# Products over the whole TensorE array, earlier weight conversions and experts in a written order, in a fused attention, gated FFN and mixture-of-experts kernel

## The chip, the core and the metric

The kernel runs on one core of one Trainium2 chip. The core has five engines with an instruction queue each: TensorE (PE, matrix products; its loads of the stationary operand are listed as PEld), VectorE (DVE), ScalarE (ACT), GpSimd (POOL) and SyncE (SP, which here only issues DMA transfers). An engine works through its queue in order, and instructions of different engines are tied together by semaphores. The metric is the device time of one execution. Before the change it is 1046.84 us, the median of three runs (1045.98, 1046.84 and 1047.32). All times below are microseconds (us) unless a nanosecond is named.

## The reference

Three stages, each feeding the next, in fp32:

```
x = attention(q, k, v)        # 4 batches x 8 heads x 576 positions x 64, block-causal (blocks of 64)
x = x as [2304, 512]          # 4*576 tokens
x = (sigmoid(x @ w_gate) * (x @ w_val)) @ w_out       # 512 -> 1536 -> 512
logits = x @ moe2_w_gate                              # 8 experts
# capacity assignment: walk all (token, expert) pairs in descending order of logit;
# a token takes the expert if it has none yet and the expert holds fewer than 288 tokens
out[tokens of e] = relu(x[tokens of e] @ w1[e]) @ w2[e]      # 512 -> 1024 -> 512, 288 tokens each
```

## The kernel before

Every large fp32 product is made of three faster ones: both operands are split into a high part and the rest (`xh`, `xl`, `w0h`, `w0l`, `ewh`, `ewl`: ACT writes the high part, DVE or POOL subtracts), and high x high, high x low and low x high are added up in PSUM. A PSUM tile is called `A` whatever it holds.

**Stage 1, 0 to 78 us: attention of batch 0.** Heads go in pairs; each pair takes five row blocks. PE makes scores and transposes `p`, DVE reduces maxima and sums (`stat`) and copies (`pta`, `ptb`, `kf`), ACT exponentiates, POOL scales `p` and splits the result (`xh` L218, `xl` L219). Beside it the first FFN weights are made ready (`Ffn.start`, `Ffn.convert` L339): they come as 64-bit numbers, and `ToF32` makes fp32 of one tile of 128x512 by one ACT instruction (L283) and four DVE ones (L288, L290, L292, L294). ACT and POOL then split it (`w0h` and `w1h` L357, `w0l` and `w1l` L359). `first_half` (L1115) interleaves the two generators.

**Stage 2, 78 to 573 us: the first FFN product** (L457) with the attention of batches 1 to 3 woven in. `router_weights` (L556 to L570) also computes the product w_out @ m_gate there, so that the router logits (`logits` L410, `rows` L425) come from the FFN's hidden values without waiting for its second product.

**Stage 3, 573 to 784 us: the second FFN product** (`Ffn2.run`, L683: 18 token tiles) and beside it the router. `Router.phase` (L815) finds, seven times over, a threshold for each expert by a search in two halves of three steps. A step compares all keys with J candidates (`cmp`, L840 or L845; J is 31 or 63 or 64), counts on PE by 18 products of `cmp` with the one-hot experts `oh` (L824, bf16, J columns of the array), makes flags on DVE (`ge` L831), and adds them up on PE (L834, J rows of the array, and in the last step of a phase L837). `FILL` says how many L683 products stand between. The output rows go to DRAM through `x2r` (L690) as two halves of 256 columns.

**Stage 4, 784 to 1044 us: the experts.** For each: POOL fetches the expert's tokens by indirect DMA (`gather` L997, three token tiles of 128, 128 and 32, two halves each, one expert ahead), `xtrans` (L1009) transposes them on PE, L1049 is the product with w1, L1090 that with w2, `ytrans` (L1023) transposes the result back, and POOL scatters it by three indirect DMAs (L1030). Eight weight chunks per expert are loaded by SP into `eraw` (3 buffers) and split by `split` (L958: `ewh` on ACT, two instructions `ewl` on DVE or POOL, in turn) into a ring of 5. In this version all of stage 4 goes through the scheduler, which places each instruction by its own costs; the code order is only a hint.

## Time and profile before

| | us |
|---|---|
| median of three runs | 1046.84 |
| the profiled execution | 1045.71 |
| its span, first to last instruction | 1044.0 |
| PE busy | 993.2 (95%) |
| DVE, ACT, POOL busy | 587.7, 449.7, 507.4 (56%, 43%, 49%) |
| mean granted TensorE clock | 0.985 of full |

The span is what the trace covers; the device time is 1.7 us longer. A busy share says little on its own: PE is busy 95% of the span, so that a change has to take work from PE, or one of its few waits, to move the time. A timeline row gives the start, the duration from start to end, and in brackets how long the engine was idle before and which instruction it waited for. PE's products overlap in the pipeline: the time that one costs is the distance from its start to the next start, not its duration.

### The profile page before, as it was taken

What the parts mean: (1) busy time and instruction counts of PE and PEld (TensorE: products, weight loads), DVE (VectorE), ACT (ScalarE), POOL (GpSimd) and SP (SyncE); (2) the same over time, 40 slices, a digit from 0 to 9 for tenths busy, and PEclk for the clock granted to TensorE, in tenths of its full rate; (3) what the DMA queues carried; (4) which work ended last, traced back from release to release, by engine and by line L of the source; (5) the groups of instructions that cost most, each with busy time, mean ns of one, the idle gap of its engine ahead of it and who ended that gap; (6) DMA issues with size and microseconds to landing.
All of it is one profiled execution on the core that took longest, in us unless ns stands there. A gap on an engine that the chain in (4) does not pass through costs nothing.

```text
span 1044.0 us, 19724 instructions
## 1 busy us (share of the span) xinstructions
PE 993.2 (95%) x7387; PEld 858.1 (82%) x7387; DVE 587.7 (56%) x1385; ACT 449.7 (43%) x1069; POOL 507.4 (49%) x519
## 2 busy tenths in 40 slices
PE   7979999999999999999999999999997999999995
PEld 4658888788888888899999766666687999999995
DVE  5887889477666455435685566655631434434441
ACT  5765565355554455434554222111121444444541
POOL 3663444433333334532324677765645666666441
PEclk9989999999999999998999999999998999999998
DMA  6556666556454322236665543433312665555540
GB/s 170 141 130 176 203 199 178 181 165 185 142 184 119 96 68 79 75 98 226 207 210 157 148 126 102 119 84 96 98 47 63 205 186 174 177 169 183 185 127 23
DMA packets 188527, 148.89 MB, mean 143 GB/s; under 512 B 70800, under 2 KB 161424, under 8 KB 188432
## 3 DMA queue, kind: packets, MB, share of 16 engines
q1 hardware_dynamic: 184848, 138.20, 44.5%
q0 software_dynamic: 3584, 9.44, 2.8%
q8 instruction: 58, 0.95, 0.4%
q14 instruction: 37, 0.30, 0.1%
HBM read 114.57 MB, written 33.03 MB: 141 GB/s over the span
## 4 chain that ended last, share of the span: by engine, by line
PE 84%; DVE 8%; issue 4%; POOL 1%; ACT 1%; SPq 1%; DMA 0%; POOLq 0%; another core or an unknown queue 0%; ACTq 0%; DVEq 0%
PE A L457 29%; PE A L683 12%; PE A L1049 10%; PE A L1090 9%; PE A L211 5%; PE A L116 4%; PE A L163 4%; PE A L824 2%; PE A L410 2%; DVE sub L811 2%; PE A L122 2%; PE A L1009 1%; PE A L85 1%; DVE cmp L840 1%; DVE hl L512 1%
## 5 line engine op out<-in xcount | busy, mean ns | idle before, releaser
L151 POOL TENSOR_SCALAR p<-p,stat 128x128 f32<-128x128 f32 (+2 forms) x144 | 81.2, 576 | 191.1 <-DVE stat L149 135.8
L359 POOL TENSOR_TENSOR w0l<-wf,w0h 128x512 fp32r<-128x512 f32 x48 | 67.0, 1395 | 136.9 <-ACT w0h L357 103.4
L457 PE MATMUL A<-xh,w0h 128*128 128x288 f32 x384 | 121.6, 317 | 2.6 <-ACT w0h L357 2.6
L457 PE MATMUL A<-xh,w1h 128*128 128x288 f32 x384 | 122.1, 318 | 1.9 <-ACT ptb L168 1.9
L976 POOL TENSOR_TENSOR ewl<-eraw,ewh 128x512 fp32r<-128x512 f32 x68 | 90.2, 1345 | 63.1 <-ACT ewh L969 55.6
L457 PE MATMUL A<-xh,w0l 128*128 128x288 f32 x384 | 114.5, 298 | 3.7 <-POOL w0l L359 3.7
L457 PE MATMUL A<-xh,w1l 128*128 128x288 f32 x384 | 114.3, 298 | 0.0
L457 PE MATMUL A<-xl,w1h 128*128 128x288 f32 x384 | 114.3, 298 | 0.0
L457 PE MATMUL A<-xl,w0h 128*128 128x288 f32 x384 | 114.1, 297 | 0.0
L969 ACT ACTIVATE ewh<-eraw 128x1024 fp32r<-128x1024 f32 x64 | 67.8, 1060 | 67.2 <-PE A L1090 42.0
L124 DVE TENSOR_REDUCE stat<-A 128x1 f32<-128x128 f32 (+4 forms) x160 | 70.4, 477 | 44.2 <-PE A L122 20.5
L683 PE MATMUL A<-wo_h,hl 128*128 128x512 f32 (+1 forms) x240 | 95.0, 396 | 0.0
L683 PE MATMUL A<-wo_l,hh 128*128 128x512 f32 (+1 forms) x240 | 92.1, 384 | 0.0
L660 POOL TENSOR_TENSOR hl<-hraw,hh 128x512 fp32r<-128x512 f32 x54 | 75.8, 1426 | 28.7 <-ACT hh L656 28.7
L683 PE MATMUL A<-wo_h,hh 128*128 128x512 f32 (+1 forms) x240 | 89.7, 374 | 0.0
L974 DVE TENSOR_TENSOR ewl<-eraw,ewh 128x512 fp32r<-128x512 f32 x60 | 48.6, 851 | 70.8 <-ACT ewh L969 64.9
L138 ACT ACTIVATE p<-A,stat 128x128 f32<-128x128 f32 (+4 forms) x160 | 81.8, 520 | 11.7 <-DVE stat L124 7.5
L690 ACT ACTIVATE x2r<-A 128x512 f32<-128x512 f32 (+1 forms) x20 | 11.1, 555 | 168.2 <-PE A L683 162.6
L1049 PE MATMUL A<-exh,ewh 128*128 128x288 f32 x256 | 75.9, 314 | 6.0 <-issue 3.3
L457 PEld LDWEIGHTS A<-xh,w1h 128*128 128x128 f32 x384 | 73.5, 191 | 9.0 <-issue 5.1
L457 PEld LDWEIGHTS A<-xh,w0h 128*128 128x128 f32 x384 | 73.1, 190 | 8.7 <-issue 4.4
L1049 PE MATMUL A<-exl,ewh 128*128 128x288 f32 x256 | 75.8, 299 | 2.3 <-issue 2.3
(219 smaller groups left out, 2717.1 us busy)
## 6 DMA issues: line engine op xcount, KB each, us to landing
eraw<-in_moe_w_dram SPq DMA_DIRECT2D x64, 512.0 KB, 3.9
wf<-wgv SPq DMA_DIRECT2D x72, 256.0 KB, 3.0
h<-h SPq DMA_DIRECT2D x48, 288.0 KB, 2.7
hraw<-h SPq DMA_DIRECT2D x16, 768.0 KB, 5.2
hraw<-h SPq DMA_DIRECT2D x12, 576.0 KB, 4.0
w<-in_moe_w_gate_dram SPq DMA_DIRECT2D x12, 512.0 KB, 4.3
w<-in_moe_w_val_dram SPq DMA_DIRECT2D x12, 512.0 KB, 4.1
wgv<-wf SPq DMA_DIRECT2D x24, 256.0 KB, 4.3
```

The lines of the kernel that those rows point to most:

```text
L124: nc.vector.tensor_reduce(st[:, x:x + 1], s[:, 0:w], axis=AX.X, op=OP.max, negate=True)
L138: nc.scalar.activation(o, s[:, 0:w], AF.Exp, bias=m, scale=1.0, accum_out=st[:, 2 + x:3 + x])
L151: self.k.mark = nc.gpsimd.tensor_scalar(t, t, r[:, x:x + 1], 1.0, op0=OP.mult, op1=OP.mult)
L211: nc.tensor.matmul(o[64 * a:64 * a + 64, b0:w], vs[0:kk, c, a, :], th[0:kk, a, c, b0:w], start=(n == 0), stop=(n == len(mm) - 1))
L359: nc.gpsimd.tensor_tensor(l, x, f32(h), op=OP.subtract)
L457: nc.tensor.matmul(o[:, 0:288], w[:, ks], x[:, ts], start=(kk == 0 and n == 0), stop=(kk == 3 and n == 2))
L660: nc.gpsimd.tensor_tensor(l[:, s], x[:, s], f32(h[:, s]), op=OP.subtract)
L683: nc.tensor.matmul(o[:, 0:b - a], x[:, f], w[:, f, a:b], start=(f == 0 and n == 0), stop=(f == 11 and n == 2))
L969: nc.scalar.activation(h, x, AF.Copy)
L976: nc.gpsimd.tensor_tensor(l[:, s], x[:, s], f32(h[:, s]), op=OP.subtract)
L1049: nc.tensor.matmul(o[:, 0:288], w[:, s], x, start=(d == 0 and n == 0), stop=(d == 3 and n == 2))
L1090: nc.tensor.matmul(o[:, 0:288], w[:, s], x, start=(n == 0), stop=(n == 23))
```

## The change

Four parts.

1. **Whole-array products.** Router counts, flags, router weights, logit rows and the third token tile of `xtrans` used 16, 31, 32, 40, 63 or 64 rows or columns of the array. Now each uses 128 x 128; what is added is zero or is not read. For this the tiles are widened and cleared once by POOL (`memset`, `affine_select`).
2. **First conversions.** `first_half` advances the weight conversion at every attention step after the second, not at every third.
3. **Experts in a written order.** Stage 4 stands under `tc.manual_schedule()`, so that its instructions keep the order of the code. The code is reordered for that: splits begin one step earlier, five of eight are split by DVE and three by POOL (four and four before); the transposes of the next expert stand in the middle of each w2 product; the back transposes and the scatters of an expert stand in the first three steps of the next one; for the last expert nine of twelve back transposes go ahead of the last product's end.
4. **Gather.** The FFN's output is stored twice, as halves (`x2_h`, which only expert 0 fetches) and as whole rows (`x2_d`). The other experts are fetched by three indirect DMAs of 2 KB rows in place of six of 1 KB rows, 128 rows each, padding included.

```diff
@@ first_half
-        n += s1.step > 2
-        if n % 3 == 1:
+        if s1.step > 2:
             next(w0, None)
@@ router_weights
-    mgs = k.const.tile([P, 4, 16], F32R, name="mgs")
+    mgs = k.const.tile([P, 4, P], F32R, name="mgs")
+    nc.gpsimd.memset(f32(mgs), 0.0)
...
-                nc.tensor.matmul(o[0:16, 0:256], mgs[:, c, :], x[:, c, :], ...)
+                nc.tensor.matmul(o[:, 0:256], mgs[:, c, :], x[:, c, :], ...)
...
-            nc.tensor.transpose(o[:, 16 * y:16 * y + 16], ot[:, P * y:P * y + P], k.ident[0:16, 0:16])
+            nc.tensor.transpose(o[:, P * y:P * y + P], ot[:, P * y:P * y + P], k.ident)
@@ Ffn2.run
-                nc.sync.dma_start(k.x2_d[c // 256][t * P:(t + 1) * P, :], y[:, c - a:c - a + 256])
+                nc.sync.dma_start(k.x2_h[c // 256][t * P:(t + 1) * P, :], y[:, c - a:c - a + 256])
+            nc.sync.dma_start(k.x2_d[t * P:(t + 1) * P, a:b], y[:, 0:b - a])
@@ Router.phase
-                    nc.tensor.matmul(o[0:J, 0:8], self.cmp[:, c * J:c * J + J], self.oh[:, c, :],
+                    nc.tensor.matmul(o[:, 0:8], self.cmp[:, c * J:c * J + P], self.oh[:, c, :],
...
-                nc.tensor.matmul(base[:, 0:1], self.wgt[h, s][0:J], self.fl[0:J], ...)
+                nc.tensor.matmul(base[:, 0:1], self.wgt[h, s], self.fl, ...)
...
-                    nc.tensor.matmul(o[:, 16:24], self.ones[0:J, :], self.ge[0:J], start=True, stop=True)
+                    nc.tensor.matmul(o[:, 16:24], self.ones, self.ge, start=True, stop=True)
@@ Experts
-EARLY = 5
+EARLY = 6
@@ xtrans
-                nc.tensor.transpose(o[:, a:b], self.gx[e, j][0:b - a, d * P:(d + 1) * P], k.ident[0:b - a, 0:b - a])
+                nc.tensor.transpose(o[:, a:a + P], self.gx[e][j][:, d * P:(d + 1) * P], k.ident)
@@ run
+                if f % 2 == 0:
+                    drain(bg)
+                    if e or f:
+                        bg = self.split("vg"[f // 2 % 2])
+                    next(bg, None)
...
-                if f % 2 == 1:
-                    drain(bg)
-                    bg = self.split("v" if f % 4 == 1 else "g")
...
-                bg = self.split("v" if d % 2 == 1 else "g")
+                bg = self.split("gv"[d % 2] if d else "v")
...
+                    if f == 3:
+                        next(nxt, None)
+                        if e == 7 and d == 3:
+                            drain(self.rows(e, yt, (0, 1, 2), False))
@@ kernel
-    ex.gather(0)
-    drain(ex.run())
+    with tc.manual_schedule():
+        ex.gather(0)
+        ex.run()
```

DVE before, in the attention of the fourth head pair of batch 0: `w` and `cv_t` rows are conversions of FFN weights, the others belong to the attention.

```order
L294 SCALAR_TENSOR_TENSOR wf_864<-w_311,cv_t 128x512
L170 COPY pta<-A 128x4x128
L146 TENSOR_SCALAR stat<-stat 128x2
L149 RECIPROCAL stat<-stat 128x2
L124 TENSOR_REDUCE stat<-A 128x1 x2
L288 TENSOR_SCALAR w_338<-w_338 128x512
L290 TENSOR_SCALAR cv_t<-cv_t 128x512
L292 SCALAR_TENSOR_TENSOR cv_t<-cv_t,w_338 128x512
L294 SCALAR_TENSOR_TENSOR wf_1035<-w_338,cv_t 128x512
L288 TENSOR_SCALAR w_381<-w_381 128x512
```

DVE now, at the first conversion, in the first head pair:

```order
L124 TENSOR_REDUCE stat<-A 128x1 x2
L288 TENSOR_SCALAR w_287<-w_287 128x512
L290 TENSOR_SCALAR cv_t<-cv_t 128x512
L170 COPY ptb<-A 128x4x128
L146 TENSOR_SCALAR stat<-stat 128x2
L149 RECIPROCAL stat<-stat 128x2
L90 COPY kf<-A 128x512
L124 TENSOR_REDUCE stat<-A 128x1 x2
L292 SCALAR_TENSOR_TENSOR cv_t<-cv_t,w_287 128x512
L294 SCALAR_TENSOR_TENSOR wf_380<-w_287,cv_t 128x512
L170 COPY ptb<-A 64x2x64
```

The four conversions of the first weights, of which two stood in a row at the end, now lie two instructions per attention step over the first three pairs; the place of the first piece in the fourth pair holds attention alone.

POOL before, in one expert (`xg` a gather, `out_dram` a scatter):

```order
L997 DMA xg_11257<-x2d_63,idx 128x256
L997 DMA xg_11257<-x2d_64,idx 128x256
L997 DMA xg_11259<-x2d_63,idx 128x256
L997 DMA xg_11261<-x2d_63,idx 32x256
L997 DMA xg_11259<-x2d_64,idx 128x256
L997 DMA xg_11261<-x2d_64,idx 32x256
L1030 DMA out_dram<-yr_10923,idx 2304x512
L1030 DMA out_dram<-yr_10970,idx 2304x512
L976 TENSOR_TENSOR ewl<-eraw,ewh 128x512 x2
L1030 DMA out_dram<-yr_11019,idx 2304x512
L976 TENSOR_TENSOR ewl<-eraw,ewh 128x512 x6
```

And now:

```order
L1011 DMA xg_10550<-x2d,idx 128x512
L1011 DMA xg_10551<-x2d,idx 128x512
L1011 DMA xg_10552<-x2d,idx 128x512
L1051 DMA out_dram<-yr_10579,idx 2304x512
L1050 MEMSET one 1x1
L1051 DMA out_dram<-yr_10580,idx 2304x512
L1050 MEMSET one 1x1
L1051 DMA out_dram<-yr_10581,idx 2304x512
L985 TENSOR_TENSOR ewl<-eraw,ewh 128x512 x6
```

Three of nine indirect DMAs and one of four splits are gone from POOL's queue, and every split stands behind all of them.

PE before, where one expert's w2 product (L1090) ends and the next expert's w1 product (L1049) begins:

```order
L1090 MATMUL A<-eh_9982,ewl 128x288
L1009 MATMUL A<-ident,xg_9858 128x128
L1009 MATMUL A<-ident,xg_9860 128x128
L1009 MATMUL A<-ident,xg_9862 128x32
L1009 MATMUL A<-ident,xg_9858 128x128
L1009 MATMUL A<-ident,xg_9860 128x128
L1009 MATMUL A<-ident,xg_9862 128x32
L1049 MATMUL A<-exh_10066,ewh 128x288
```

And now, in the middle of the last of the four w2 products (L1118):

```order
L1118 MATMUL A<-eh_9943,ewl 128x288
L1023 MATMUL A<-ident,xg_9897 128x128
L1023 MATMUL A<-ident,xg_9898 128x128
L1023 MATMUL A<-ident,xg_9899 128x128
L1118 MATMUL A<-eh_9959,ewh 128x288
```

The last transposes of the next expert's tokens no longer stand right ahead of the products that read them, and the third is as wide as the others.

## Rows read from the trace of the kernel before

**Rows 1.** The page, shares of the chain that ended last, by engine.

```profile
PE 84%; DVE 8%; issue 4%; POOL 1%; ACT 1%; SPq 1%; DMA 0%; POOLq 0%; another core or an unknown queue 0%; ACTq 0%; DVEq 0%
```

**Rows 2.** Windows (start:end length, busy us and count per engine, PE clock, DMA).

```profile
26.42:38.14 11.72, 11.72 (x93) 7.72 (x95) 8.72 (x27) 9.25 (x31) 7.28 (x14) 1.00 0.73 177
38.14:50.49 12.35, 11.79 (x93) 7.71 (x95) 11.03 (x31) 8.69 (x30) 8.07 (x13) 1.00 0.35 88
...
73.44:77.60 4.16, 4.16 (x19) 3.80 (x19) 3.41 (x6) 1.49 (x4) 1.82 (x2) 0.50 0.56 170
```

**Rows 3.** Timeline of PE at the first FFN products.

```profile
69.26 0.40 PE L457 MATMUL A<-xh,w0h 128*128 128x288 f32 x1 [2.64 <-ACT w0h L357]
...
73.44 0.61 PE L457 MATMUL A<-xh,w0l 128*128 128x288 f32 x1 [3.66 <-POOL w0l L359]
```

**Rows 4.** Timeline of POOL in the same stretch.

```profile
70.81 1.17 POOL L219 TENSOR_TENSOR xl<-xr,xh 128x320 fp32r<-128x320 f32 x1
```

**Rows 5.** Timeline of PE in a router phase, narrow products between L683.

```profile
591.72 0.74 PE L824 MATMUL A<-oneh,cmp 128*63 128x8 bf16 x18
...
592.97 0.40 PE L683 MATMUL A<-wo_l,hh 128*128 128x512 f32 x1
593.30 0.17 PE L834 MATMUL A<-flag,wgt 63*128 63x1 bf16 x1
...
593.75 0.39 PE L683 MATMUL A<-wo_h,hh 128*128 128x512 f32 x1
...
595.13 0.39 PE L683 MATMUL A<-wo_h,hh 128*128 128x512 f32 x1
595.45 0.61 PE L824 MATMUL A<-oneh,cmp 128*31 128x8 bf16 x18
...
596.33 0.40 PE L683 MATMUL A<-wo_h,hl 128*128 128x512 f32 x1
```

**Rows 6.** Timeline of PE, two whole-array bf16 products between L683.

```profile
681.39 0.39 PE L683 MATMUL A<-wo_h,hl 128*128 128x512 f32 x1
681.62 0.18 PE L863 MATMUL A<-row,ones 128*128 128x1 bf16 x1
...
682.00 0.40 PE L683 MATMUL A<-wo_l,hh 128*128 128x512 f32 x1
```

**Rows 7.** Timeline of PE, whole-array bf16 products with 48 columns moving.

```profile
765.88 0.32 PE L920 MATMUL A<-cmp,ohlo 128*128 128x48 bf16 x6
```

**Rows 8.** Waits of PE, 573 to 768 us (us in total, times, longest).

```profile
PE A L834 <- DVE ge L831: 3.9, 7, 0.7
```

**Rows 9.** Timeline of PE at the start of the experts.

```profile
788.25 1.45 PE L1049 MATMUL A<-exh,ewh 128*128 128x288 f32 x5 [2.69 <-ACT exh L1012]
...
797.70 1.05 PE L1049 MATMUL A<-exh,ewh 128*128 128x288 f32 x6 [2.22 <-issue]
```

**Rows 10.** Windows of single experts: the second and, without gathers, the sixth.

```profile
855.14:885.37 30.23, 29.50 (x219) 28.26 (x218) 12.93 (x23) 13.87 (x25) 18.91 (x18) 1.00 0.58 179
...
976.92:1006.00 29.08, 29.08 (x219) 28.17 (x218) 12.10 (x24) 14.06 (x25) 12.98 (x11) 1.00 0.54 166
```

**Rows 11.** Timeline of PE, both kinds of transposes between expert products.

```profile
875.38 0.56 PE L1009 MATMUL A<-ident,xg 128*128 128x128 f32 x3
...
876.10 0.30 PE L1090 MATMUL A<-el,ewh 128*128 128x288 f32 x1
```

**Rows 12.** The same view, the full transposes.

```profile
884.88 0.49 PE L1023 MATMUL A<-ident,yt 128*128 128x128 f32 x3
...
885.35 0.30 PE L1049 MATMUL A<-exl,ewh 128*128 128x288 f32 x1
```

**Rows 13.** Waits of PE, 784 to 1044 us.

```profile
PE A L1049 <- issue: 7.1, 12, 2.2
```

**Rows 14.** Waits of all engines, 825 to 1006 us.

```profile
ACT ewh L969 <- DMA eraw<-in_moe_w_dram: 4.0, 3, 1.8
```

**Rows 15.** Timeline of POOL, one of an expert's nine indirect DMAs.

```profile
855.11 0.97 POOL L997 DMA_INDIRECT xg<-x2d,idx  x1 [0.30 <-issue]
```

More of the change, by code (lines that the diff above doesn't have):

```diff
@@ L540, in router_weights @@
     mg = k.const.tile([P, 4, 8], F32, name="mg")
-    mgs = k.const.tile([P, 4, 16], F32R, name="mgs")
+    mgs = k.const.tile([P, 4, P], F32R, name="mgs")
+    nc.gpsimd.memset(f32(mgs), 0.0)
+    ots = [ffn.cv.tile([P, 256], F32, name=f"wot{i}", bufs=1) for i in range(2)]
+    for ot in ots:
+        nc.gpsimd.memset(ot, 0.0)
     nc.sync.dma_start(mg, k.m_gate.rearrange("(k p) e -> p k e", p=P))
@@ L555, in product @@
             for x in (xh, xl):
-                nc.tensor.matmul(o[0:16, 0:256], mgs[:, c, :], x[:, c, :], start=(c == 0 and x is xh), stop=(c == 3 and x is xl))
-        ot = ffn.cv.tile([16, 256], F32, name="wot", bufs=1)
-        nc.scalar.activation(ot, o[0:16, 0:256], AF.Copy)
+                nc.tensor.matmul(o[:, 0:256], mgs[:, c, :], x[:, c, :], start=(c == 0 and x is xh), stop=(c == 3 and x is xl))
+        ot = ots[f // 2 % 2]
+        nc.scalar.activation(ot[0:16], o[0:16, 0:256], AF.Copy)
         for _ in range(GAP):
@@ L987, in open @@
         self.hb = st.enter_context(tc.tile_pool(name="ehb", bufs=1))
+        self.one = self.hb.tile([1, 1], F32, name="one")
     def gather(self, e):
@@ L992, in gather @@
             return
[L993 removed]
+        self.gx[e] = [self.xg.tile([P, 512], F32, name=f"xg{j}") for j in range(3)]
+        for src in k.x2_h if e == 0 else (k.x2_d,):
             for j, (a, b) in enumerate(self.TOK):
[L995 to L998 removed]
+                g = self.gx[e][j]
+                if e == 0:
+                    c = k.x2_h.index(src)
+                    g = g[:, 256 * c:256 * c + 256]
+                nc.gpsimd.indirect_dma_start(out=g, out_offset=None, in_=src[:, :],
+                                             in_offset=bass.IndirectOffsetOnAxis(ap=k.idx[:, 3 * e + j:3 * e + j + 1], axis=0))
     def xtrans(self, e):
@@ L1015, in xtrans, with rows @@
             yield
-    def ytrans(self, e, yt):
+    def rows(self, e, yt, ds, copies):
         k, nc = self.k, self.k.nc
+        if not self.yo:
+            self.yo = [k.psA.tile([P, 512], F32, name="A") for _ in self.TOK]
+            self.yr = [self.yg.tile([P, 512], F32, name=f"yr{j}") for j in range(3)]
+        lo, hi = ds[0] * P, ds[-1] * P + P
         for j, (a, b) in enumerate(self.TOK):
-            n = b - a
-            o = k.psA.tile([P, 512], F32, name="A")
-            for d in range(4):
-                nc.tensor.transpose(o[0:n, d * P:(d + 1) * P], yt[d][:, a:b], k.ident)
-            r = self.yg.tile([P, 512], F32, name=f"yr{j}")
+            o = self.yo[j]
+            for d in ds:
+                nc.tensor.transpose(o[0:b - a, d * P:(d + 1) * P], yt[d][:, a:b], k.ident)
+            r = self.yr[j][0:b - a]
             if j == 0:
-                nc.scalar.activation(r[0:n], o[0:n], AF.Copy)
+                nc.scalar.activation(r[:, lo:hi], o[0:b - a, lo:hi], AF.Copy)
             else:
-                nc.vector.tensor_copy(r[0:n], o[0:n])
-            yield
-            s = nc.gpsimd.indirect_dma_start(out=k.out[:, :], out_offset=bass.IndirectOffsetOnAxis(
-                ap=k.idx[0:n, 3 * e + j:3 * e + j + 1], axis=0), in_=r[0:n, :], in_offset=None)
-            for x in self.sent:
-                k.tc.declare_no_dep(s.ins, x.ins, reason="no token is in two slots")
-            self.sent.append(s)
-            yield
+                nc.vector.tensor_copy(r[:, lo:hi], o[0:b - a, lo:hi])
+            if copies:
+                if j:
+                    nc.gpsimd.memset(self.one, 0.0)
+                s = nc.gpsimd.indirect_dma_start(out=k.out[:, :], out_offset=bass.IndirectOffsetOnAxis(
+                    ap=k.idx[0:b - a, 3 * e + j:3 * e + j + 1], axis=0), in_=r, in_offset=None)
+                for x in self.sent:
+                    k.tc.declare_no_dep(s.ins, x.ins, reason="no token is in two slots")
+                self.sent.append(s)
+            yield
+        if copies:
+            self.yo = []
     def run(self):
         k, nc = self.k, self.k.nc
+        self.yo = []
         nxt = self.xtrans(0)
-        tail, bg = iter(()), iter(())
+        tail = iter(())
         early = {}
@@ L1072, in run @@
                 next(tail, None)
[L1073 to L1075 removed]
                 next(bg, None)
+            drain(tail)
             yt = []
@@ L1096, in run @@
                 yt.append(y)
-                if d >= 1:
-                    next(nxt, None)
+            drain(bg)
             drain(nxt)
-            drain(tail)
-            tail = self.ytrans(e, yt)
-            yield
+            tail = self.rows(e, yt, range(4) if e < 7 else (3,), True)
         drain(tail)
@@ L1176, in tile_fn @@
     k.wo_d = dram.tile([12, P, 512], F32, name="wo32")
-    k.x2_d = [dram.tile([2304, 256], F32, name=f"x2d{c}") for c in range(2)]
+    k.x2_d = dram.tile([2304, 512], F32, name="x2d")
+    k.x2_h = [dram.tile([2304, 256], F32, name=f"x2h{c}") for c in range(2)]
     const = k.const = ctx.enter_context(tc.tile_pool(name="const", bufs=1))
```

37 lines of the change are left out of this document (17 added, 20 removed).

## The prediction, made before the changed kernel was run

> **What bounds the kernel now.** I read first the shares of the chain of waits: PE is 84% of it, DVE 8%, nothing else over 4% [rows 1]. So a microsecond taken off PE's queue counts, unless DVE was late in that place anyway. Then the windows, stage by stage, for PE's holes and its clock; there the reader should see that the attention pairs between 26 and 50 us keep PE full but not DVE, and that just before 77 us PE runs at clock 0.50 [rows 2]. Then PE's own timeline around the holes [rows 3, 9] and around the narrow products [rows 5, 6, 11, 12], and last the lists of what PE waits for [rows 8, 13]. The sum below is against the profiled execution, 1045.71 us, which lies 1.13 under the median of 1046.84.
>
> **1. First conversions.** PE stands 2.64 us before the first product with `w0h` and 3.66 before the first with `w0l`: 6.3 together [rows 3]. After that it runs 4.16 us at 0.50 of its clock [rows 2]; that is the lower of the two levels, after a stretch in which it had hardly worked, and costs another 2.1. The pair at 38 to 50 us lasts 12.35 in place of 11.72, with one conversion in it: 0.6 [rows 2]. In all 9.0. In the new order the four conversions are done before the fourth pair, so `w0h` is no longer late. What is late next is `w0l`: POOL has the attention's `xl` in its queue until 70.81 + 1.17 = 71.98 [rows 4], some 1 us after the second product could want it. So 8.0 can go.
>
> Against it stands DVE in the first pairs. It is busy 8.72 of 11.72 without, and 11.03 with, one conversion; a conversion is worth 2.3 [rows 2]. Two in a pair make 8.7 + 4.6 = 13.3, 1.6 more than the pair lasts, in two pairs: 3.2 if all of it reaches PE. ACT, at 9.25 [rows 2], is nearer to its limit as well. Nothing hides that, as every attention step reads DVE's sums; a part may be made good in the third pair. I take 8 - 3 = **-5**, bounds -9 (no loss) and 0 (the loss is twice as large, and a second of the waits stays).
>
> **2. Router weights and logit rows.** The 48 products with 16 columns and 12 small transposes come in six bursts each, the logit rows in four. At each border between a narrow and a wide shape PE pays what is priced in part 3, 0.1 to 0.2. Against it stands POOL, which clears two tiles once. **-1**, bounds -3 and +2 (POOL's clearing holds up the attention's `p`).
>
> **3. Router counts and flags.** A 512-column L683 takes (595.13 - 593.75)/6 = 0.23 us. From the L683 before an insertion to the second L683 after it are two of these and the insertion. So 18 products of 31 columns cost 596.33 - 595.13 - 0.46 = 0.74, and one L834 costs 593.75 - 592.97 - 0.46 = 0.32, for a product of a single column [rows 5]. Two whole-array products of that size cost 682.00 - 681.39 - 0.46 = 0.15 together [rows 6]. Thus the narrow shape, not the product, is what costs, about 0.2 at the borders. 63 columns: 0.74 within the group against 0.61 for 31 [rows 5], so 0.87.
>
> What will 18 whole-array products cost? Six of L920 lie within 0.32 [rows 7], one product within 0.18 [rows 6]: (0.32 - 0.18)/5 = 28 ns each, though 48 columns move. By the same division 31 columns cost (0.61 - 0.18)/17 = 25 ns and 63 cost 33 [rows 5]. I take 25 to 28, so 18 x 0.026 and 0.09 for the borders = 0.55. Saved: 28 groups of 31 x 0.19 = 5.3, 14 groups of 63 or 64 x 0.32 = 4.5, 42 flags x 0.22 = 9.2: 19 us of PE time, 2.7 per phase.
>
> The Trainium skill ("TensorE: Matmul & The Clock Gate", LDWEIGHTS) speaks against this: the load of the stationary operand takes time by its columns, P/1.2 ns, whatever its rows. By it 18 loads of 128 columns would be 18 x 97/1.2 = 1455 ns longer than those of 31, an estimate from that page, and the change would lose; L920's 28 ns per product [rows 7] do not agree. The same skill ("TensorEngine Tiling (Array Packing)", Key Properties) says that a change of tiling mode drains TensorE; the dearer narrow flag agrees with that.
>
> How much of the 19 reaches the end? Where PE waits for DVE, time saved before the wait only makes it longer. PE waits for `ge` seven times, 3.9 us, once per phase [rows 8]: DVE is last in one of the two halves. What is saved in that half I count as lost, the other half keeps: **-10**, bounds -19 (all of it) and -3 (DVE late in nearly every step).
>
> **4. Start of the experts.** PE stands 2.69 us for `exh` and later 2.22 [rows 9]. The first wait has a chain that stays: last `x2r`, store, gather, transpose, ACT. The second can shrink, since expert 0's second halves are no longer fetched behind expert 1's first ones, and 36 products rather than 30 lie ready. But SP has a store more per tile and the third gather is of 128 rows. **-2**, bounds -5 and +2.
>
> **5. Experts.** Three transposes with a 32-row third cost from their start to the start of the second product after them 876.10 - 875.38 = 0.72 [rows 11], three full ones 885.35 - 884.88 = 0.47 [rows 12]. There are 32 such groups: 32 x 0.25 = 8.0. PE works without a break here, so all of it counts. Besides, PE waits 7.1 us on "issue" before L1049 in twelve places [rows 13]; the sixth expert, the one without gathers, has none of it, 29.08 us against 30.23 [rows 10]. The wait lies behind POOL's indirect DMAs, 1.27 us each from one to the next [rows 15]: nine per expert are 11.4, and the splits of the first chunks queue behind them. Six make 7.6, DVE takes a fifth split and each split begins earlier: I take 4 of the 7.1 as gained. **-12**, bounds -15 and 0 (in order, ACT or POOL delays the products by what the transposes give back). An expert should last 30.2 - 1.0 - 1.0 = 28.2, or near 28.1, the 29.08 of the sixth less 1.0. The last scatters stay in the tail: 0.
>
> **Sum.** -5 - 1 - 10 - 2 - 12 = -30: 1045.7 - 30 = 1015.7 by the profiled execution, and 1.1 more against the median: 1017 us.
>
> **Rivals.**
>
> *Whole-array loads are dear.* For it: in the groups the price grows with the columns, 25 ns at 31 and 33 at 63 [rows 5]. Going on by 8 ns for 32 columns, 128 columns cost 49 ns. Then a group takes 18 x 0.049 + 0.09 = 0.97: 28 x 0.23 + 14 x 0.10 = 7.8 lost against 9.2 gained at the flags. Part 3 falls to -1: 1026. Against it: the 28 ns of L920. The Trainium skill's rule on the columns, given in part 3, points the same way, and further.
>
> *The router is DVE's.* For it: the waits of PE in each phase [rows 8], and DVE as the second on the chain [rows 1]. PE's time turns into waits in both halves, part 3 is -3: 1024. Against it: in one half no such waits are listed.
>
> *The written order stalls the experts (slower than before).* ACT must take its queue in order: `ewh` of a chunk that SP has not yet landed holds up the `eh` behind it, which frees PE's PSUM tiles and feeds the w2 product. Even before, `ewh` waited for its load three times, 1.3 us each [rows 14]. The scheduler could put another instruction first; the written order can't. With 64 chunks, the gains of 30 us are eaten when each costs PE 0.5 us more; at 0.75 the time is 1047 - 30 + 48 = 1065. Against it: ACT is busy 13.87 of 30.23 us [rows 10], so that a wait of 1 us per chunk fits into its idle time, and splits are five chunks ahead.
>
> *It does not do what it says:* the freed waits are taken up elsewhere and every part falls on its bad bound: 0 + 2 - 3 + 2 + 0 = +1, 1048.
>
> **How the numbers follow.** The forecast gets 0.66 (own range 1004 to 1024), dear loads 0.13, the router bound by DVE 0.13, stalled experts 0.05, nothing gained 0.03. The lower end has parts 1, 3 and 4 half way to their good bounds (-2, -4.5, -1.5) and parts 2 and 5 at theirs (-2, -3): 13 below, 1004. The upper end has the dear loads (+9), no gain at the first conversions (+5) and a third less in the experts (+4): 18 above, 1035. A measurement of this kernel tells about 0.2%, 2.1 us, from no change. Faster by more: 0.92; within it: 0.03; slower: 0.05.
>
> **What would show it.** Right: no wait of PE over 1.5 us between 66 and 77 us; 18 counts within 0.65 us on PE's timeline, and flags followed by an L683 after 0.3; experts of 28.2 us with PE busy nearly all of it; transposes of the third tile without a gap. Wrong: counts of 0.9 us or more (dear loads); waits for `ge` or `cmp` that have doubled (DVE); rows of PE in the experts that wait for `eh`, `ewh` or `ewl` for more than 1 us per expert; attention pairs of more than 13 us.

## The result and the profile after

The changed kernel takes 1016.77 us (median of four runs, 1012.12 to 1019.31) against 1046.41 beside it: a ratio of 0.9712 with an interval of 0.9671 to 0.9753, 2.9% or 30 us less. Forecast were 1017 and a range of 1004 to 1035. Timed again on another chip it takes 1015.88, but there the kernel before takes only 1033.47 (0.9825, 0.981 to 0.984): 18 us less. So there are two kinds of chip here: on the first the kernel before takes 1045 to 1046 us, on the second 1033. What differs lies in the kernel before, and its cause stays open. The profiled execution of the changed kernel took 1014.82 us, with a span of 1013.0.

The page of the changed kernel, busy time and the shares of the chain by engine (the latter answers to [rows 1]):

```profile
PE 966.7 (95%) x7387; PEld 844.6 (83%) x7387; DVE 601.2 (59%) x1399; ACT 455.9 (45%) x1070; POOL 477.3 (47%) x514
...
PE 78%; DVE 11%; DMA 3%; issue 3%; SPq 1%; ACT 1%; POOL 1%; POOLq 0%; ACTq 0%; DVEq 0%
```

PE has 26.5 us less work (966.7 for 993.2) in as many products, up to 6.8 of them by the clock (below), and its share of the chain went to DVE and DMA: it waits for these more than before.

Both kernels issue the same 7387 products on PE and in most stages in the same order, so the start of the n-th product can be set beside its start in the other trace. The difference between two such points tells what a stage gained (the numbers below are such starts and their differences). "Other chips" sets the changed kernel's second profile (experiment 5) against that of the kernel before with the conversions alone changed (experiment 1); both ran on chips of the second kind.

| stage (products) | before | after | gained | other chips | forecast |
|---|---|---|---|---|---|
| attention of batch 0 and start (to 480) | 82.58 | 80.64 | 1.9 | (see the experiments) | 5 |
| first FFN product (480 to 4100) | 494.38 | 492.46 | 1.9 | 0.7 | 1 |
| router (4100 to 5600) | 200.41 | 193.23 | 7.2 | 8.2 | 10 |
| start of the experts (5600 to 5800) | 35.72 | 29.96 | 5.8 | -0.4 | 2 |
| experts (5800 to 7386) | 219.74 | 207.62 | 12.1 | 6.1 | 12 |
| last product to the end | 11.13 | 9.11 | 2.0 | 2.0 | 0 |
| span | 1044.0 | 1013.0 | 31.0 | | 30 |

Part of the small differences is the clock: the trace of before has six stretches at the lower of the two levels ahead of its end (five of 3.4 us and one of 6.8), that of after three of 3.4. A stretch of 3.4 us costs at most half its length, 1.7 us. In the router's stage, where the first trace of the changed kernel has one and the second has none, it costs 1.0 (193.2 and 192.2). The stretches differ from run to run of the same kernel: the five runs of the second timing went from 1012.4 us at a mean clock of 0.996 to 1017.3 at 0.989.

*First products of the FFN.* PE's timeline of the changed kernel, the products that had the waits in [rows 3]:

```profile
73.55 0.40 PE L457 MATMUL A<-xh,w0h 128*128 128x288 f32 x1
73.79 0.29 PE L457 MATMUL A<-xl,w0h 128*128 128x288 f32 x1
73.92 0.29 PE L457 MATMUL A<-xh,w0l 128*128 128x288 f32 x1
```

No wait and no half clock is left there. But the products start 4.3 us later than in [rows 3]: the time was lost in the first three head pairs. PE's timeline, the product (L211) that ended each of the windows in [rows 2]:

```profile
29.27 3.43 PE L211 MATMUL A<-ptb,vraw 128*64 128x320 f32 x20
...
43.31 2.16 PE L211 MATMUL A<-ptb,vraw 128*64 128x320 f32 x16
...
57.42 2.42 PE L211 MATMUL A<-ptb,vraw 128*64 128x320 f32 x20
```

The first stands 2.9 us later than before, and the two pairs behind it last 14.0 and 14.1 us in place of 11.7 and 12.4. More than 13 us was named by the forecast as a sign of being wrong. The first loss is seen in SP's, DVE's and PE's timelines:

```profile
21.01 0.59 SPq L331 DMA_DIRECT2D w<-in_moe_w_gate_dram  x1
```

```profile
25.10 0.43 DVE L288 TENSOR_SCALAR w<-w 128x512 int32<-128x512 uint32 x1 [1.94 <-DMA w<-in_moe_w_gate_dram]
```

```profile
26.32 0.30 PE L163 MATMUL A<-ident,p 128*64 128x128 f32 x1 [1.10 <-ACT ptb L168]
```

The load of the first weights is issued at 21.01 and its readers start at 25.10. ACT and DVE reach the conversion before it and stand there, with the attention's copies behind them, and PE waits for such a copy (`ptb`). From 27.9 us the clock is at its lower level for 3.4 us, in which the L211 at 29.27 takes 3.43 in place of 2.42.

*Router.* PE's timeline of the changed kernel, answering to [rows 5]:

```profile
587.29 0.40 PE L687 MATMUL A<-wo_l,hh 128*128 128x512 f32 x1
587.53 0.18 PE L846 MATMUL A<-flag,wgt 128*128 128x1 bf16 x1
...
587.88 0.40 PE L687 MATMUL A<-wo_h,hh 128*128 128x512 f32 x1
...
589.26 0.39 PE L687 MATMUL A<-wo_h,hh 128*128 128x512 f32 x1
589.50 0.61 PE L836 MATMUL A<-oneh,cmp 128*128 128x8 bf16 x18
...
590.27 0.39 PE L687 MATMUL A<-wo_h,hl 128*128 128x512 f32 x1
...
591.70 0.16 PE L846 MATMUL A<-flag,wgt 128*128 128x1 bf16 x1 [0.80 <-DVE ge L843]
```

By the reckoning of the forecast (two products of 0.23 taken off) the 18 counts cost 590.27 - 589.26 - 0.46 = 0.55, as forecast, and the flag 587.88 - 587.29 - 0.46 = 0.13 in place of 0.32. The last row shows the other side. PE's waits from 560 to 765 us, answering to [rows 8]:

```profile
PE A L846 <- DVE ge L843: 6.5, 7, 1.2
PE A L836 <- DVE cmp L852: 4.0, 8, 0.6
PE A L836 <- DVE oneh L805: 1.6, 2, 0.8
PE A L875 <- DVE q L869: 1.0, 2, 0.6
PE A L932 <- DVE ohlo L927: 0.9, 2, 0.5
```

The wait for `ge` grew from 3.9 to 6.5 us, and one for `q` is new, 1.0. That for `cmp` grew to 4.0; before it was

```profile
PE A L824 <- DVE cmp L840: 2.1, 7, 0.6
```

*Experts.* The window of one expert, answering to [rows 10], and a group of three transposes, to [rows 11]:

```profile
834.31:862.40 28.09, 28.09 (x219) 28.02 (x218) 13.52 (x25) 14.88 (x25) 13.96 (x15) 1.00 0.64 200
```

```profile
821.79 0.49 PE L1023 MATMUL A<-ident,xg 128*128 128x128 f32 x3
...
822.25 0.29 PE L1118 MATMUL A<-el,ewh 128*128 128x288 f32 x1
```

An expert lasts 28.09 us with PE busy for all of it (forecast 28.1 to 28.2), and the group takes 822.25 - 821.79 = 0.46 in place of 0.72. The twelve waits of [rows 13] are gone: this is the whole list of PE's waits from 765 us on.

```profile
PE A L1023 <- DMA xg<-x2h,idx: 2.4, 2, 1.4
PE A L1042 <- ACT yt L1127: 0.6, 1, 0.6
PE A L1073 <- ACT exh L1026: 0.3, 2, 0.2
```

### The profile page after: what moved, and what is told of

It reads as the page before. It is cut to its first block, busy times and chain, and to the rows that moved or that the text cites. A ratio compares the mean times of both kernels' runs of the same rounds, so it can differ in the third digit from the quotient of the medians.

```text
span 1013.0 us, 19715 instructions
## 1 busy us (share of the span) xinstructions
PE 966.7 (95%) x7387; PEld 844.6 (83%) x7387; DVE 601.2 (59%) x1399; ACT 455.9 (45%) x1070; POOL 477.3 (47%) x514
## 4 chain that ended last, share of the span: by engine, by line
PE 78%; DVE 11%; DMA 3%; issue 3%; SPq 1%; ACT 1%; POOL 1%; POOLq 0%; ACTq 0%; DVEq 0%
PE A L457 27%; PE A L687 10%; PE A L1073 9%; PE A L1118 9%; PE A L211 4%; PE A L116 4%; PE A L163 4%; DVE cmp L852 2%; PE A L836 2%; PE A L122 2%; DVE sub L823 2%; PE A L410 2%; PE A L85 1%; DMA hraw<-h 1%; DVE hl L512 1%
## 5 line engine op out<-in xcount | busy, mean ns | idle before, releaser
L359 POOL TENSOR_TENSOR w0l<-wf,w0h 128x512 fp32r<-128x512 f32 x48 | 64.9, 1353 | 135.1 <-ACT w0h L357 110.9
L985 POOL TENSOR_TENSOR ewl<-eraw,ewh 128x512 fp32r<-128x512 f32 x56 | 75.0, 1358 | 67.6 <-ACT ewh L981 67.4
L1118 PE MATMUL A<-eh,ewh 128*128 128x288 f32 x256 | 78.0, 305 | 0.0
L470 DVE SCALAR_TENSOR_TENSOR h<-sg,A 128x288 f32<-128x288 f32 x96 | 43.1, 449 | 58.3 <-PE A L457 41.3
L1118 PE MATMUL A<-eh,ewl 128*128 128x288 f32 x256 | 75.9, 297 | 0.0
```

The source lines that it names most:

```text
L359: nc.gpsimd.tensor_tensor(l, x, f32(h), op=OP.subtract)
L470: nc.vector.scalar_tensor_tensor(h[:, ts], sg, 1.0, ps[1][:, 0:288], op0=OP.add, op1=OP.mult)
L985: (nc.vector if eng == "v" else nc.gpsimd).tensor_tensor(l[:, s], x[:, s], f32(h[:, s]), op=OP.subtract)
L1118: nc.tensor.matmul(o[:, 0:288], w[:, s], x, start=(n == 0), stop=(n == 23))
```

## The experiments

The median of the kernel before, run beside each experiment, was 1033.5 for the first four, 1033.5 for the next four, 1045.4 for the following three and 1033.2 for the last.

**1. The conversions alone**, in the kernel before.

```diff
-        n += s1.step > 2
-        if n % 3 == 1:
+        if s1.step > 2:
             next(w0, None)
```

> The kernel before with one edit of the change, the conversions at each attention step. In the trace of the changed kernel PE is 7.0 us later than before at the end of the fifth head pair and 1.9 us earlier from 80 us on, since the 9 us of waits and half clock at the first FFN products are gone. If that is this edit alone, the time falls by 2 us, to about 1044.5, PE shows waits in the first three pairs that add up to about 7 us with a half-clock stretch, and none before w0h and w0l. The prediction's sum says -5 (1041.5). If DVE's load took all of the gain, the time stays at 1046.5.

1031.37 against 1033.54, ratio 0.9981 (0.9971 to 0.9991): 1 to 3 us less. In the trace product 300 starts at 56.95 (before: 50.42, 6.5 late) and product 480 at 80.16 (before: 82.58, 2.4 early). So the stage's 1.9 us are this edit's, and the gain is less than half of the forecast's 5. The 9 us of waits and clock were rightly read: from product 300 to 480 23.2 us pass in place of 32.2. The half-clock stretch that was expected in the first pairs is not in this trace, and PE is 6.5 us behind without it.

This trace also shows the experts of the kernel before, with their code unchanged, on a chip where PE has no waits on issue there. The window of its second expert, answering to [rows 10]:

```profile
844.64:873.71 29.07, 29.07 (x217) 28.16 (x217) 12.57 (x22) 14.06 (x26) 19.25 (x17) 1.00 0.61 186
```

29.07 us with its gathers, as long as the sixth expert in [rows 10] without them.

**2. The conversions two steps later**, in the changed kernel.

```diff
-        if s1.step > 2:
+        if s1.step > 4:
```

> The changed kernel with the conversions from the fifth attention step on in place of the third. Theory: 2.7 of the 7.0 us lost in the pairs come from the first conversion alone, because its load, issued at 21 us, lands at 25.1, and ACT and DVE stand before it in their queues; PE then waits 1.1 us and runs 3.4 us at the lower clock level. Two steps later the load has landed: PE is 4.3 us behind in the place of 7.0 and the time falls by 2 to 3 us, to about 1014. Rival: the loss is DVE's load wherever the conversions stand; then PE is 7 us behind as before and the time is unchanged (1016.8), or worse if w0h is late again.

Product 300 starts at 54.78, 4.4 us behind before in place of 7.0, and PE's wait for `ptb` is gone: the 2.7 us belong to the load, as expected. Little of them is the clock, as experiment 1, without the stretch, is 6.5 behind. Up to product 480 the kernel is 2.0 us ahead of the changed one. The median, 1015.92 (ratio 0.9818, 0.9796 to 0.9841), does not tell it from the changed kernel on such a chip, 1015.88; 2 to 3 us less were expected. The runs of either spread over 5 to 7 us. PE's path shows a gain, in one trace of each; the time does not show it.

**3. The router's products narrow again**, in the changed kernel.

```diff
-                    nc.tensor.matmul(o[:, 0:8], self.cmp[:, c * J:c * J + P], self.oh[:, c, :], ...)
+                    nc.tensor.matmul(o[0:J, 0:8], self.cmp[:, c * J:c * J + J], self.oh[:, c, :], ...)
-                nc.tensor.matmul(base[:, 0:1], self.wgt[h, s], self.fl, ...)
+                nc.tensor.matmul(base[:, 0:1], self.wgt[h, s][0:J], self.fl[0:J], ...)
-                    nc.tensor.matmul(o[:, 16:24], self.ones, self.ge, start=True, stop=True)
+                    nc.tensor.matmul(o[:, 16:24], self.ones[0:J, :], self.ge[0:J], start=True, stop=True)
```

> The changed kernel with the router's counts, flags and the product behind the flags on J columns and rows again, all else as changed. By the two traces the stage of the router gave back 7.2 us (PE's lead grew from 3.9 to 11.0 us), so the time should rise by 7, to about 1024. If all of the saved PE time had counted it would rise by 19; if the router were bound by DVE in nearly every step, by 3; if wide loads were dear, not at all.

1022.73 (0.9894, 0.988 to 0.9909): 6.9 us above the changed kernel. From product 4100 to 5600 it takes 200.2 us, as before (200.4), and the changed kernel on that kind of chip 192.2. Its waits from 560 to 765 us are those of [rows 8] to the tenth:

```profile
PE A L846 <- DVE ge L843: 3.9, 7, 0.7
PE A L836 <- DVE cmp L852: 2.1, 7, 0.6
```

Wide loads are not dear. The windows of the stage, narrow here and wide in the changed kernel's second profile, neither with a stretch at the lower clock:

```profile
572.58:772.81 200.23, 191.37 (x1501) 139.25 (x1500) 117.69 (x333) 40.10 (x71) 129.98 (x88) 1.00 0.43 123
574.67:766.85 192.18, 177.78 (x1502) 132.36 (x1500) 122.71 (x333) 40.09 (x71) 130.64 (x88) 1.00 0.45 128
```

PE is busy 191.37 us in place of 177.78 and idle 8.9 in place of 14.4. So the wide products save 13.6 us of PE time, not 19, and the waits that grew take 5.5 of it; 8 are left, and nothing is missing. By the forecast's reckoning, less PE's idle time in each place, the 42 groups of counts cost 33.5 us narrow and 26.8 wide, and the 42 flags, with the seven products behind them, 13.4 and 6.8. That saves 6.7 and 6.6, where 9.8 and 9.2 were forecast. The price of 0.55 holds for 18 of the 42 wide groups; the other 24 cost 0.60 to 0.72. That of 0.13 holds for 28 of the flags; the seven that had to wait for `ge` cost 0.28 besides the wait.

**4. Other numbers of FFN products between the router's steps**, in the changed kernel.

```diff
-FILL = (((13, 6), (4, 3), (6, 3)), ((8, 3), (4, 3), (6, 3)), 10)
+FILL = (((13, 6), (7, 3), (6, 3)), ((8, 7), (5, 3), (6, 3)), 10)
```

> The changed kernel with other numbers of FFN products between the router's steps: 7 for 4 ahead of the second count of the first half, 7 for 3 between the first count and its flags in the second half, 5 for 4 ahead of its second count; 8 products more per phase, 56 in all, which come from the stretch after the router. Theory: what the whole-array shapes freed beyond 7 us stands in PE's waits for ge (6.5 us) and cmp (4.0 us), because DVE is last there. Products put into those waits cost nothing: waits near 1 us in all, time down by 8 to 9 us, to 1008. Rival: the router's own chain gets longer by the products, and the waits come back one step later: time unchanged or up by a few us.

1014.36 (0.9804, 0.979 to 0.9817): at most 1.5 us less than the changed kernel's 1015.9, not 8, and not beyond the spread of the runs. From product 4100 to 5658, the last of the second FFN product, 197.6 us pass, 1.5 less than the changed kernel's 199.1, and up to 3.2 less if one counts out a stretch at the lower clock, at 757 us. The waits from 560 to 768 us:

```profile
PE A L836 <- DVE oneh L805: 3.3, 4, 0.8
PE A L846 <- DVE ge L843: 2.7, 4, 1.5
PE A L902 <- DVE t L904: 2.6, 1, 2.6
PE A L836 <- DVE cmp L852: 1.7, 5, 0.5
PE A L875 <- DVE q L869: 0.4, 1, 0.4
```

The waits for `ge` and `cmp` shrank from 10.5 to 4.4, those for `oneh` doubled, and after the last phase stands a new one of 2.6; in all they are 10.7 in place of 14.0. My theory, by which 1 us of waits was to be left, fell, and the rival is nearer. It sees the router as a chain of PE's and DVE's steps in turn, where a product put in the way lengthens the chain by about what the wait got shorter.

**5. The changed kernel once more.**

> The changed kernel itself once more, unedited. The kernel before took 1046.4 us where the change was first timed and 1033.5 us on the chip of the first four experiments, whose trace (with one edit in the attention) shows none of PE's waits on issue in the experts. Theory: those waits, some 7 us, and 5 us of the start of the experts belong to the old order of stage 4 on some chips only, and the changed kernel hasn't got them on either; then it takes 1014 to 1018 us here too and the gain is 1.7%. Rival: the whole program is faster on this chip; then the changed kernel takes about 1004.

1015.88, beside a before of 1033.47. The changed kernel is as fast on both kinds of chip (1016.77 and 1015.88); the kernel before is not. Its second profile has experts of 28.08 and 28.23 us in turn, as the first.

**6. The third token tile 32 rows again**, in the changed kernel.

```diff
-                nc.tensor.transpose(o[:, a:a + P], self.gx[e][j][:, d * P:(d + 1) * P], k.ident)
+                nc.tensor.transpose(o[:, a:b], self.gx[e][j][0:b - a, d * P:(d + 1) * P], k.ident[0:b - a, 0:b - a])
```

> The changed kernel with the third token tile transposed from 32 rows again (32 groups of three), all else as changed. By the rows of before, 0.25 us per group come back: the time rises by 8 us against the changed kernel. If PE had slack in the experts, the rise is under 3.

1022.46 (0.9902, 0.9884 to 0.9921), 6.6 us above. From product 5800 to the last it takes 214.59 against 207.61: 6.98 us for the 27 groups of three there, 0.259 each. PE's timeline shows the same place as above, where now 0.72 us pass:

```profile
821.84 0.55 PE L1023 MATMUL A<-ident,xg 128*128 128x128 f32 x3
...
822.56 0.30 PE L1118 MATMUL A<-el,ewh 128*128 128x288 f32 x1
```

The forecast's 0.25 per group holds, and PE has no slack there that could hide it. Of its 32 groups 28 count; the first expert's four stand among PE's waits for its gathers. Narrow, the experts last 29.1 and 29.3 us in turn; those of the kernel before on such a chip last 29.1 and 29.2 (experiment 1). So on these chips nothing else in the change makes an expert shorter: neither order nor gathers nor splits.

**7. The scheduler's order for stage 4**, with the changed code.

```diff
-    with tc.manual_schedule():
-        ex.gather(0)
-        ex.run()
+    ex.gather(0)
+    ex.run()
```

> The changed kernel without the written order: the scheduler places stage 4, from the same code. Theory: the written order is worth the waits before the first product of an expert; on a chip where before has none of those waits it is worth little, and the time rises by 0 to 2 us. If the order itself matters (transposes close to their readers, late splits), it rises by 4 to 6.

1017.1 (0.9847, 0.9834 to 0.986), 1.2 above the changed kernel and within the spread; its profiled span is 1013.0 against 1014.1, and product 5800 to the last takes 207.6 us in both. The written order is worth nothing measurable here. It was run only on a chip of the second kind.

**8. Six gathers per expert**, in the changed kernel.

```diff
-        for src in k.x2_h if e == 0 else (k.x2_d,):
+        for src in k.x2_h:
...
-                if e == 0:
-                    c = k.x2_h.index(src)
-                    g = g[:, 256 * c:256 * c + 256]
+                c = k.x2_h.index(src)
+                g = g[:, 256 * c:256 * c + 256]
```

> The changed kernel with six gathers of 1 KB rows per expert in place of three of 2 KB. The prediction blamed POOL's indirect DMAs for PE's waits on issue: nine per expert again, 3.8 us more in POOL's queue ahead of the three splits. If that is right, waits of PE of about 0.5 us per expert come back, 4 us in all. Rival: splits five chunks ahead hide it, and the time is unchanged within 1 us.

The waits did not come back. POOL's timeline shows the nine indirect DMAs in a row, and the first split behind them (from the gather at 841.48 on):

```profile
841.48 0.95 POOL L1010 DMA_INDIRECT xg<-x2h,idx  x1 [0.30 <-issue]
842.73 1.00 POOL L1050 DMA_INDIRECT out_dram<-yr,idx  x1 [0.30 <-issue]
...
845.33 0.86 POOL L1050 DMA_INDIRECT out_dram<-yr,idx  x1 [0.22 <-DVE yr L1046]
846.22 2.54 POOL L985 TENSOR_TENSOR ewl<-eraw,ewh 128x512 fp32r<-128x512 f32 x2
```

and PE's waits from 800 us on are only that of the end:

```profile
PE A L1041 <- ACT yt L1126: 0.6, 1, 0.6
```

Product 5800 to the last takes 207.62, as with three gathers. Yet the time is 1021.05 (0.9883, 0.9868 to 0.9897), 5.2 above. 1.7 of it lie behind the last scatter, in the very end (below); the other 3.5 are not settled. Of the 4.0 us between the two profiled executions 2.5 lie between products 480 and 5600, ahead of the edit, where this one has one stretch at the lower clock more and one twice as long.

**9. The flags alone narrow**, in the changed kernel.

```diff
-                nc.tensor.matmul(base[:, 0:1], self.wgt[h, s], self.fl, ...)
+                nc.tensor.matmul(base[:, 0:1], self.wgt[h, s][0:J], self.fl[0:J], ...)
-                    nc.tensor.matmul(o[:, 16:24], self.ones, self.ge, start=True, stop=True)
+                    nc.tensor.matmul(o[:, 16:24], self.ones[0:J, :], self.ge[0:J], start=True, stop=True)
```

> The changed kernel with only the 42 flag products and the 7 products behind them on J rows again; the counts stay on 128 columns. The prediction put 9.2 of its 19 us of PE time there. Undoing counts and flags together cost 8.2 us on PE's path between two points of the traces and 7 us in the median. If the two halves count alike, flags alone cost about 4 us of this stage (median near 1020); if the flags, whose wait for ge is the one that DVE ends, are hidden, under 1.5; if they are all of it, 8.

1020.77 (0.9772, 0.9756 to 0.9788), on a chip where before takes 1045.4; 4 us more than the changed kernel's 1016.77 beside such a before, half of what undoing all of it costs. On PE's path it takes 195.8 from product 4100 to 5600, against 193.2 in the first trace of the changed kernel, each with one stretch at the lower clock there: 2.6, a third of the 8. So the flags are a third of it by the path and somewhat over half by the time; that they count just as much as the counts is not shown.

**10. The conversions later and thinner**, in the changed kernel.

```diff
+    n = 0
     while s1.done < 3:
         next(att, None)
-        if s1.step > 2:
+        n += s1.step > 4
+        if n % 3:
             next(w0, None)
```

> The changed kernel with the conversions from the fifth attention step on and at two of three steps. With them from the fifth step at every step PE was 4.4 us behind at the end of the fifth pair. Theory: that rest is DVE's excess, two conversions of 2.3 us in pairs that have 3.0 to spare; spread over three pairs they fit. PE is then at most 1.5 us behind and w0h still in time: 3 us less than the 1015.9 of both kernels, 1013. Rival: the loss comes from the place of each conversion ahead of the attention's own copies, however thin they are spread: PE stays 4 us behind, and the time at 1016.

Product 300 starts at 52.19, 1.8 us behind before; with every step from the fifth it was 4.4. Of the 4.4 spreading takes away 2.6, which speaks for DVE's excess; 1.8 stay, a little more than the 1.5 expected, and may be the rival's. `w0h` is in time, and what is late is `w0l`, by the 1 us that the forecast read from [rows 4]:

```profile
70.44 0.40 PE L457 MATMUL A<-xh,w0l 128*128 128x288 f32 x1 [1.16 <-POOL w0l L359]
```

Product 480 starts 3.3 us earlier than in the changed kernel, 1.3 earlier than in experiment 2: half of the 2.6 is spent again by then. The median, 1014.02 (0.9702, 0.9681 to 0.9724), is the lowest here, but 2.7 under the changed kernel's beside such a before is not more than the runs spread; the profile has six stretches at the lower clock.

**11. The same with the router's products distributed otherwise.**

```diff
-FILL = (((13, 6), (4, 3), (6, 3)), ((8, 3), (4, 3), (6, 3)), 10)
-FIRST, TAIL = 8, (15, 35)
+FILL = (((13, 6), (6, 3), (6, 3)), ((8, 6), (4, 3), (6, 3)), 10)
+FIRST, TAIL = 8, (22, 35)
```

> As the one before, and with other numbers of FFN products in the router: 6 for 4 ahead of the second count of the first half, 6 for 3 ahead of the flags of the second half's first step, 22 for 15 after the last phase, where the earlier attempt (56 products more) got a new wait of 2.6 us and gave back only 2.4 us of PE's path. Theory: with 35 products in the phases and 7 behind them the waits for cmp and ge halve and no new one comes: 4 us less than the pace alone, 1009. Rival: the router's chain is as long as the products that stand in it, what is put in comes back as a wait further on: 1012 to 1013.

1018.07 (0.9736, 0.9718 to 0.9753), 4 us slower than without. From product 4100 to 5600 it takes 197.5 us against 193.2 (each with a stretch at the lower clock), and the waits are 15.5 us in place of 14.0:

```profile
PE A L846 <- DVE ge L843: 5.9, 7, 1.6
PE A L836 <- DVE oneh L805: 3.3, 4, 0.8
PE A L836 <- DVE cmp L852: 3.2, 10, 0.5
PE A L932 <- DVE ohlo L927: 2.1, 3, 1.0
PE A L875 <- DVE q L869: 1.0, 1, 1.0
```

A miss, and worse than the rival. The numbers also set when the splits of the next token tile, which run on POOL and ACT beside the router, are issued; whether that is the reason was not tried.

**12. Three gathers alone**, in the kernel before (expert 0 keeps its halves; whole rows are stored as well).

```diff
+            nc.sync.dma_start(k.x2_w[t * P:(t + 1) * P, a:b], y[:, 0:b - a])
...
                 if c == 0:
                     self.gx[e, j] = self.xg.tile([P, 512], F32, name=f"xg{j}")
-                nc.gpsimd.indirect_dma_start(out=self.gx[e, j][0:b - a, 256 * c:256 * c + 256], out_offset=None, in_=k.x2_d[c][:, :],
+                elif e:
+                    continue
+                g = self.gx[e, j][0:b - a]
+                nc.gpsimd.indirect_dma_start(out=g if e else g[:, 256 * c:256 * c + 256], out_offset=None,
+                                             in_=k.x2_w[:, :] if e else k.x2_d[c][:, :],
...
+    k.x2_w = dram.tile([2304, 512], F32, name="x2w")
```

> The kernel before with one edit of the change: whole rows stored as well, and three gathers of 2 KB rows per expert in place of six (expert 0 keeps its halves); shapes, order and splits as before. On some chips before takes 1045 to 1046 us, with 1.2 to 1.7 us of waits of PE per expert (issue) at products whose ACT copies come late while POOL issues its gathers; on others 1033.5, without them. Theory: the nine indirect DMAs bring them, as the sixth expert of before, without gathers, has none. Then this kernel takes 1034 or less on a chip of the first kind, and on one of the second only the end gets shorter, by 1.7 us (from the last scatter to the end 5.8 in place of 7.6), to 1032. Rival: they come from the narrow transposes or the scheduler's order; then PE's waits stay on a chip of the first kind and the time is 1043 to 1045.

It ran on a chip of the second kind: 1032.05 against 1033.22, ratio 0.9992 (0.998 to 1.0003), no difference beyond noise, and in the trace the shorter end that was expected. Whether the gathers cause the waits on chips of the first kind it could not show there.

## Why the prediction was right, point by point

**What bounds the kernel:** right. On the other chips, in two traces with three stretches at the lower clock each (experiments 1 and 5), PE's busy time falls by 21.1 us (988.5 to 967.4): 13.6 of them in the router and 7 in the experts (experiments 3 and 6). The span falls by 15.5. Most of what was saved away from waits for DVE came through; in the router 5.5 turned into such waits (experiment 3).

**First conversions, -5:** the direction right, the size wrong; measured are -1 to -3. The gain came, 9 where 8 was forecast: PE does not wait for `w0l` either, whose 1 us shows only with the conversions later and thinner (experiment 10). The term that failed is the loss, "1.6 more than the pair lasts, in two pairs: 3.2". It is 7.0 on PE's path. 2.7 of it is a wait that I had not listed, of the first conversion for its own load (experiment 2). The other 4.4 lie in the two pairs, 14.0 and 14.1 us long where 13.3 was reckoned. I had named DVE and priced it by busy time alone. Spreading the same work takes away 2.6 of the 4.4 (experiment 10); that the rest is the delay of the copies behind each conversion is likely, but not shown.

**Router weights and logit rows, -1:** 1.9 between the two first traces, 0.7 between two that have as many stretches at the lower clock.

**Router counts and flags, -10:** 7.2 and 8.2 on PE's path, 6.9 in the time when undone. The mechanism was right, and its two factors were too large both ways. The PE time saved is 13.6 us and not 19, since the prices read in one place (0.55 per group, as forecast, and 0.13 per flag for 0.10) do not hold in all (experiment 3). And of the 13.6 the waits took 5.5, less than the half that was taken off. The rival "whole-array loads are dear" is out: 18 products with loads of 128 columns lie within 0.61 us, as those of 31 did [rows 5]. The rival of a router bound by DVE is true in part, as the waits for `ge` and `cmp` grew by 4.5 us, but 8 were left and not 3. The Trainium skill ("TensorE: Matmul & The Clock Gate", LDWEIGHTS) has loads take time by their columns, and no such price appears here. The Trainium skill's rule on the drain between tiling modes ("TensorEngine Tiling (Array Packing)", Key Properties) agrees with the 0.19 us that a flag lost by going to the whole array.

**Start of the experts, -2:** -5.8 on the first pair of traces, of which up to 3.4 are two stretches at the lower clock that the changed kernel lacks; +0.4 on the other chips. On the first, the second wait of [rows 9] is gone. That expert 0's order of gathers took it away, as forecast, is not shown: experiment 1 has the old order without that wait, and there nothing was gained.

**Experts, -12:** the sum right (12.1), one of its two terms right in its cause. The transposes: 0.25 per group forecast, 0.259 measured, in 28 groups of 32, 7.2 us. The 4 us of the waits on issue: the forecast took them out of 7.1 [rows 13], but 3.1 of these stand at the start of the experts, among them the 2.22 that its part 4 had counted already, and 4.0 in the experts. All went. But the reason that I gave, POOL's indirect DMAs ahead of the splits, is refuted where it could be tried: nine DMAs per expert bring no wait there (experiment 8), and the kernel before, with nine, has none on that chip either (experiment 1). On the first chip ACT's copies came late in those places, with nothing in the trace to hold them: in the expert of [rows 10] the first `eh` starts at 861.02, 3.82 us behind the copy `yr`, and in experiment 1 it starts 2.35 behind it. Which part of the change took that away, and what it is, stays open; none of the runs that would tell fell on such a chip.

**Tail, 0:** 2.0, of which 0.3 lie between the last transposes and the first scatter (0.6 us in place of 1.0) and 1.7 behind the last scatter, in the end of the program.

**The rival of a slower written order:** did not come; `ewh` and `eh` hold up nothing, and between 806 and 975 us no wait of `ewh` for its load [rows 14] is listed any more.

So the total is right partly by luck: 3 us too much at the conversions and 3 at the router stand against 4 at the start of the experts and 2 at the end, which were not forecast for the reasons that brought them. And 6 of the 12 us in the experts are to be had only where the kernel before has its waits on issue; elsewhere the whole change is worth 18.

## What to carry to other kernels

A product that used part of the array, between others that use all of it, cost here by the border and not by its size. Padded with zeros, a single column went from 0.32 to 0.13 us and a group of transposes from 0.72 to 0.46. A price read in one place is not the price everywhere: over the whole router such products saved 13.6 us, not 19. In a chain that two engines pass back and forth, time saved on one comes back only in part (8 of 13.6), and shifting filler work between the steps moved the waits more than it removed them. Work that is put into an engine's in-order queue earlier should be placed after its own load has landed, and thinly enough for the engine's spare time per step. Here that was worth 2.0 and 3.3 us on PE's path, though no more in the median than the runs spread.

## What was not expected of the hardware

The kernel before takes 1045 to 1046 us on some chips and 1033 on others, with a few us between the runs on either, while the changed kernel takes 1016 on both. One chip of the second kind was timed twice, with 1033.5 and 1033.2; whether a chip always keeps to its kind is not shown. Nearly all of the difference lies in stage 4 (5800 to the last product 219.74 against 213.73 in experiment 1, and 5.6 us ahead of it, with one stretch at the lower clock more).

The end of the program goes with the number of indirect DMAs. From the start of the last scatter to the last instruction 7.55 us pass with 72 of them in the program ([rows 15] shows one) and 5.84 with 51. Three kernels' last scatters, the changed one, that with six gathers and before with three:

```profile
1007.13 0.86 POOL L1051 DMA_INDIRECT out_dram<-yr,idx  x1 [0.21 <-issue]
```

```profile
1010.55 0.86 POOL L1050 DMA_INDIRECT out_dram<-yr,idx  x1 [0.21 <-issue]
```

```profile
1024.68 0.86 POOL L1035 DMA_INDIRECT out_dram<-yr,idx  x1 [0.30 <-issue]
```

Their last instructions start at 1012.97, 1018.11 and 1030.52 us: 5.84, 7.56 and 5.84 later. The two kernels with 51 agree in spite of their different code, and the one with 72 differs from the changed kernel in the gathers alone.
